# Retention scores from whole float32 q and k, one head in each half of the array's rows

## The chip, the cores and the metric

The kernel runs on one core of one Trainium2 chip. The metric is the device time of one execution in microseconds (us). Before the change it is 1157.19 us, the median of three runs (1155.11 to 1158.36). A single run differs from another by about 0.3%.

## The reference

Three layers follow each other on 4608 tokens (8 sequences of 576) with 512 features (8 heads of 64):

```python
# retention: q, k, v are (8, 8, 576, 64)
scores = scale * np.matmul(q, k.transpose(0, 1, 3, 2))
Dmat = np.where(rel >= 0, gamma[:, None, None] ** rel, 0.0)     # rel = row - column
attn_out = np.matmul(scores * Dmat, v)
# experts: each token goes to the one expert with the largest logit
logits = x @ w_gate                                             # 512 -> 8
out[mask] = gate_w[mask, None] * (np.maximum(x[mask] @ w1[e], 0) @ w2[e])   # 512 -> 1024 -> 512
# SoLU layer
h = x @ w_in; solu = h * softmax(h); ln = layernorm(solu) * g_ln; result = ln @ w_out
```

## The kernel before, in words

The program has three stages: retention with gating and routing (about the first 250 us of the span), the experts, and the SoLU layer. The change touches the first stage only.

**Chunks.** Each sequence is cut into five chunks: four of 128 tokens (c = 0 to 3) and one of 64 (c = 4), so there are 40 chunks, numbered n. Retention runs in its chunked form. Within a chunk, the scores are k times q, multiplied by a table of decays (`dt_t`), and then by v. What came before the chunk enters through a 64x64 state per head, the sum of k times v over the earlier chunks, which is multiplied by a decayed q (`qp`). Heads are handled in four pairs: partitions 0 to 63 hold the features of the first head of a pair, 64 to 127 those of the second.

**load(n)**, L395, brings k and q (features on the partitions: `kc[:, KT]`, `kc[:, Q]`), and k and v (tokens on the partitions: `KR`, `VR`) into one tile `kc` of 1 MB. Five such tiles exist. The loads stand in the one queue of SP, and load(n+5) is asked for at the end of chunk n.

**parts(n)**, L416, makes the scores' operands. ScalarE rounds k to float32r (L427) and q to float32r (L429, two instructions, one for each half of the partitions). GpSimd subtracts k's rounded part from k (L430), VectorE q's from q (L432, two instructions). The parts of q go to `qz`, where the columns of one head hold zeros on the partitions of the other, so that one product over 128 rows gives both heads of a pair side by side. Chunks of 64 tokens have whole float32 q with zeros (`q4z`), and are not split.

**prep(n)**, L435, multiplies `KR` by its decay (L442) and makes `qp` (L449, L453), both on GpSimd.

**scores(n)**, L459: for each pair three products (rounded with rounded, rounded with rest, rest with rounded), L477, into half a bank-sized tile `ps`; after two pairs VectorE multiplies by the decay (L478) into `pp`. There are two `ps` tiles of one bank, so the products of the next half wait until L478 has read the one before the last.

**chunk(n)**, L485: `pp` times v into `po` (L494, one head in each half of the columns), the old state times `qp` added to it (L498, 128x128 with zeros outside each head's block), ScalarE copies `po` to `xts` (L506); then k times v for the pair (L511, the two blocks off the diagonal are not used), and VectorE adds the diagonal blocks to the state in SBUF (L517 for c = 0, L519).

**xtile(t)**, L525: a tile of 128 tokens is transposed and multiplied by the gate in one product per feature block (L536), two halves, each copied by ScalarE (L537). After five tiles **route(g)** is put on a list; **tick** hands out some of its small VectorE and ScalarE steps in each chunk. They pick the expert, count places, and scale the rows, which are then stored to memory.

The order on each engine is the order in which the program issues. The main loop (L699) issues for chunk n: scores(n+1), prep and parts of n+3, chunk(n), xtile, some routing steps, load(n+5); for n = 0 and 1 chunk(n) comes ahead of scores(n+1).

Of the kernel before, what the change touches and what calls it, by code (L numbers as in the profile page):

```python
# [43 lines left out]
def mk_consts():  # L44
# [4 lines left out]
    dtab = dtab.transpose(1, 0, 2)  # L49
# [30 lines left out]
def layouts(q, k, v, moe_w_gate, moe_w1, moe_w2, moe2_w_in, moe2_w_out, moe2_g_ln):  # L80
# [8 lines left out]
    def cut(a):  # L89
# [9 lines left out]
        "kt4": kt[:, :, :, n4:].reshape(B, P, -1),  # L99
        "v4": vr[:, n4:],  # L100
        "q4": qt[:, :, :, n4:].reshape(B, P, -1),
# [20 lines left out]
def kernel(ctx: ExitStack, tc, kvc, kt4, v4, q4, wg, w12, win, wout, gln,  # L122
# [60 lines left out]
    def onehots(pool, ts, ncol=NCOL, pid="pid"):  # L183
        """Per token of the tiles ts: its slot's place in a column, and its column with the token's number."""
# [41 lines left out]
    def sums(pool, a, nm):  # L226
        """Running sums of the experts' numbers in a."""
# [9 lines left out]
    def count(psum):  # L237
        """cnt: tokens per expert."""
# [121 lines left out]
    def gather(e, ts, pool, rows=NT):  # L360
        """The rows of window e's tiles ts."""
# [10 lines left out]
    with ExitStack() as ax:  # L372
        tab = ax.enter_context(tc.tile_pool(name="tab", bufs=1))
        ld = ax.enter_context(tc.tile_pool(name="ld", bufs=5))
        wk = ax.enter_context(tc.tile_pool(name="wk", bufs=2))
        ps_s = ax.enter_context(tc.tile_pool(name="ps_s", bufs=2, space=PSUM))
        ps_o = ax.enter_context(tc.tile_pool(name="ps_o", bufs=2, space=PSUM))
        ps_u = ax.enter_context(tc.tile_pool(name="ps_u", bufs=1, space=PSUM))
        ps_x = ax.enter_context(tc.tile_pool(name="ps_x", bufs=2, space=PSUM))

        NQ = 4
        NN = B * NCH
        dt_t = tab.tile([P, H, P], F32, name="dt_t")
# [3 lines left out]
        qz = [tab.tile([P, 2, NP, 2, P], F32R, name=f"qz{i}") for i in range(NQ)]  # L387
        q4z = [tab.tile([P, NP, 2, S - 4 * P], F32, name=f"q4z{i}") for i in range(2)]
        st = [tab.tile([P, NP, P], F32, name=f"st{i}") for i in range(2)]
# [5 lines left out]
        def load(n):  # L395
# [13 lines left out]
            else:  # L409
                for h2, r in enumerate(HALF):  # L410
                    nc.sync.dma_start(q4z[b % 2][r, :, h2, :], q4[b, r].rearrange("p (r j) -> p r j", r=NP))
                nc.sync.dma_start(kc[:, KT, :NP * cl], kt4[b])
                nc.sync.dma_start(kc[:cl, VR], v4[b])
            chunks[n] = [kc, None, None]

        def parts(n):  # L416
            """k and q of a full chunk in two parts; q with zeros in the place of the pair's other head."""
            if n >= NN:
                return
            b, c = divmod(n, NCH)  # L420
            if c == 4:
                return
            kc = chunks[n][0]
            z = qz[(n - b) % NQ]
            kh = wk.tile([P, 2, DM], F32R, name="kh", bufs=4)
            q = kc[:, Q].rearrange("p (r j) -> p r j", r=NP)
# [4 lines left out]
            for h2, r in enumerate(HALF):  # L431
                V.tensor_tensor(out=z[r, 1, :, h2, :], in0=q[r], in1=z[r, 0, :, h2, :].bitcast(F32), op=ALU.subtract)  # L432
            chunks[n][1] = (kh, z)

        def prep(n):  # L435
# [10 lines left out]
            if c > 0:  # L446
                qp = wk.tile([P, NP, P], F32, name="qp", bufs=4)
                if c < 4:
                    nc.gpsimd.tensor_tensor(out=qp, in0=kc[:, Q].rearrange("p (r j) -> p r j", r=NP),  # L449
                                            in1=qt_t[:, :, o - P:o], op=ALU.mult)  # L450
                else:
                    for h2, r in enumerate(HALF):
                        nc.gpsimd.tensor_tensor(out=qp[r, :, :cl], in0=q4z[b % 2][r, :, h2, :],  # L453
                                                in1=qt_t[r, :, o - P:o - P + cl], op=ALU.mult)
                chunks[n][2] = qp
# [3 lines left out]
        def scores(n):  # L459
# [5 lines left out]
            pp = wk.tile([P, H, P], F32, name="pp")  # L465
            for half in range(2):
                ps = ps_s.tile([P, 4, P], F32, name="ps")
                for i in range(2):
                    pr = 2 * half + i
                    o_ = ps[:cl, 2 * i:2 * i + 2, :cl]  # L470
                    kk = slice(pr * cl, pr * cl + cl)
                    if c == 4:
                        nc.tensor.matmul(o_, kc[:, KT, kk], q4z[b % 2][:, pr], start=True, stop=True)
                    else:
                        kh, z = chunks[n][1]
# [7 lines left out]
        free = []  # L483

        def chunk(n):  # L485
            b, c = divmod(n, NCH)
            o, cl = CHUNKS[c]
            kc, _, qp = chunks.pop(n)
            pp = pt.pop(n)
            po = ps_o.tile([P, NP, P], F32, name="po")  # L490
            for pr in range(NP):
                for h2 in range(2):
                    h = 2 * pr + h2
                    nc.tensor.matmul(po[h2 * D:h2 * D + D, pr, :cl], kc[:cl, VR, h * D:h * D + D], pp[:cl, h, :cl],  # L494
                                     start=(pr == 0), stop=(c == 0 and pr == NP - 1))
# [12 lines left out]
            if c < 4:  # L508
                pu = ps_u.tile([P, NP, P], F32, name="pu")
                for pr in range(NP):  # L510
                    nc.tensor.matmul(pu[:, pr, :], kc[:, KR, pr * P:pr * P + P], kc[:, VR, pr * P:pr * P + P],  # L511
                                     start=True, stop=True)
                old, new = st[(c + 1) % 2], st[c % 2]
                for h2 in range(2):
                    r = slice(h2 * D, h2 * D + D)
                    if c == 0:
                        V.tensor_copy(new[r, :, r], pu[r, :, r])  # L517
                    else:
                        V.tensor_tensor(out=new[r, :, r], in0=pu[r, :, r], in1=old[r, :, r], op=ALU.add)  # L519
# [5 lines left out]
        def xtile(t):  # L525
            g = max(i for i, f in enumerate(gfirst) if f <= t)
            i = t - gfirst[g]
            if i == 0:
                grp[g] = rt.tile([P, GMAX, KD, P + E], F32, name="xr", bufs=2)
            xr = grp[g]  # L530
            x = xts.pop(t)
            for half in range(2):
                px = ps_x.tile([P, 2, P + E], F32, name="px")
                for j in range(2):
                    kb = 2 * half + j
                    nc.tensor.matmul(px[:, j, :], x[:, kb, :], wgi[:, kb, :], start=True, stop=True)  # L536
                nc.scalar.copy(xr[:, i, 2 * half:2 * half + 2, :], px)  # L537
            if i == GROUPS[g] - 1:
# [115 lines left out]
        def tick(budget):  # L654
            """Some of the routing's steps; a step for the tensor engine waits for the next round."""
# [9 lines left out]
        blank = lambda i, h2: qz[i][HALF[1 - h2], :, :, h2, :]  # L665
        G = nc.gpsimd
# [537 lines left out]
```

## Time and profile before

| | |
|---|---|
| median of the runs | 1157.19 us |
| span of the profiled execution, first to last instruction | 1153.2 us |
| TensorE (PE) busy | 1091.0 us, 95% |
| VectorE (DVE) busy | 697.4 us, 60% |
| ScalarE (ACT) busy | 459.8 us, 40% |
| GpSimd (POOL) busy | 271.8 us, 24% |

The page gives no other time of the profiled execution than its span, which is 4.0 us shorter than the median of the runs. In the rows below, "x16" counts the records of a group. A float32 product leaves two records for its one instruction, and so does each loading of weights for it (PEld); a float32r product leaves one. The duration of one record of PE runs from its start to its modelled end and overlaps the next, so the pace of the array is read from one start to the next.

### The profile page before, as it was taken

How to read it: one execution, taken by the hardware profiler on the slowest of the kernel's cores; microseconds unless marked ns; L12 is line 12 of the kernel's file. 1: busy time of each engine (PE TensorE's matmuls, PEld its weight loads, DVE VectorE, ACT ScalarE, POOL GpSimd, SP SyncE). 2: the span in 40 equal slices, each digit the busy share in tenths (PEclk: the TensorE clock that was granted, in tenths of full speed). 3: DMA queues.
4: the chain of work that ended last, by engine and by line, in shares of the span. 5: the costliest groups of instructions: out<-in, count | busy, mean ns of one | idle time of the engine just before them, and what ended most of it. 6: DMA issues, size and time to landing. Idle time of an engine off the chain costs nothing.

```text
span 1153.2 us, 18685 instructions
## 1 busy us (share of the span) xinstructions
PE 1091.0 (95%) x7226; PEld 992.9 (86%) x7226; DVE 697.4 (60%) x1468; ACT 459.8 (40%) x858; POOL 271.8 (24%) x263
## 2 busy tenths in 40 slices
PE   5987989789999999999999999999999999999994
PEld 5877888779999999999999998788888888888873
DVE  8789889876333546555556664655555555555550
ACT  4444645533333333333433442433333343343330
POOL 6555555512771010101010000111111111111111
PEclk9988999999999999999999999999999999999997
DMA  8456666643444343435344332111101111010000
GB/s 292 161 176 200 214 201 211 205 131 112 145 137 148 107 159 130 166 124 176 124 154 145 134 109 78 37 55 47 48 26 55 47 46 55 19 55 28 23 24 29
DMA packets 64509, 130.76 MB, mean 113 GB/s; under 512 B 11904, under 2 KB 40320, under 8 KB 60576
## 3 DMA queue, kind: packets, MB, share of 16 engines
q1 hardware_dynamic: 39792, 101.42, 26.0%
q0 software_dynamic: 7200, 19.46, 5.3%
q10 hardware_dynamic: 17424, 8.65, 2.6%
q8 instruction: 58, 0.95, 0.3%
q14 instruction: 35, 0.29, 0.1%
HBM read 99.82 MB, written 29.68 MB: 112 GB/s over the span
## 4 chain that ended last, share of the span: by engine, by line
PE 72%; DVE 1%; issue 1%; DMA 1%; ACT 1%; POOL 0%; POOLq 0%
PE py L833 19%; PE ph L818 18%; PE phh L990 17%; PE pf L1064 15%; PE ptl L1049 2%; PE px L801 1%; DMA x<-xd,src 0%; DVE ll L1052 0%; DMA out_dram<-o__11605,dst 0%; DMA out_dram<-o__11651,dst 0%; DVE u L1012 0%; DVE nm L1000 0%; ACT lh L1051 0%; DVE u L1035 0%; ACT e__8152 L1015 0%
## 5 line engine op out<-in xcount | busy, mean ns | idle before, releaser
L833 PE MATMUL py<-hh,wh 128*128 128x344 f32 (+7 forms) x512 | 157.7, 308 | 0.0
L833 PE MATMUL py<-hl,wh 128*128 128x344 f32 (+7 forms) x512 | 154.8, 302 | 0.0
L833 PE MATMUL py<-hh,wl 128*128 128x344 f32 (+7 forms) x512 | 154.6, 302 | 0.0
L1052 DVE TENSOR_TENSOR ll<-ptl,lh 128x512 fp32r<-128x512 f32 x72 | 49.5, 688 | 105.1 <-ACT lh L1051 105.1
L990 PE MATMUL phh<-wih,yh 128*128 128x512 f32 x272 | 107.4, 395 | 1.2 <-ACT yh L974 1.2
L367 POOL DMA_INDIRECT x<-xd,src x42 | 42.4, 1008 | 277.5 <-PE px L801 216.4
L990 PE MATMUL phh<-wih,yl 128*128 128x512 f32 x272 | 106.9, 393 | 0.1
L990 PE MATMUL phh<-wil,yh 128*128 128x512 f32 x272 | 105.6, 388 | 0.0
L1029 POOL TENSOR_TENSOR rd<-v,mhalf 128x1 f32<-128x1 f32 x36 | 20.4, 565 | 356.1 <-DVE v L1027 356.1
L820 ACT ACTIVATE hh<-ph 128x344 fp32r<-128x344 f32 (+7 forms) x128 | 54.3, 425 | 121.0 <-PE ph L818 118.6
L833 PEld LDWEIGHTS py<-hh,wh 128*128 128x128 f32 x512 | 96.5, 188 | 0.1
L833 PEld LDWEIGHTS py<-hh,wl 128*128 128x128 f32 x512 | 96.5, 189 | 0.0
L833 PEld LDWEIGHTS py<-hl,wh 128*128 128x128 f32 x512 | 96.2, 188 | 0.0
L818 PE MATMUL ph<-xh,wh 128*128 128x344 f32 (+7 forms) x512 | 93.0, 303 | 1.1 <-ACT xh L804 1.1
L818 PE MATMUL ph<-xl,wh 128*128 128x344 f32 (+7 forms) x512 | 93.0, 304 | 0.0
L818 PE MATMUL ph<-xh,wl 128*128 128x344 f32 (+7 forms) x512 | 92.8, 303 | 0.0
L477 PE MATMUL ps<-qz,kh 128*128 128x256 f32 x384 | 60.7, 311 | 30.7 <-DVE pp L478 19.2
L821 DVE SCALAR_TENSOR_TENSOR hl<-ph,hh 128x344 fp32r<-128x344 f32 (+7 forms) x128 | 60.2, 472 | 48.3 <-ACT hh L820 48.0
L178 DVE TENSOR_TENSOR wl<-raw,wh 128x1024 fp32r<-128x1024 f32 x64 | 78.2, 1221 | 17.7 <-ACT wh L177 17.6
L835 ACT COPY yo<-py 128x344 f32<-128x344 f32 (+7 forms) x64 | 26.5, 413 | 142.3 <-PE py L833 111.9
L477 PEld LDWEIGHTS ps<-qz,kh 128*128 128x128 f32 x384 | 53.7, 211 | 33.3 <-issue 13.0
L1064 PE MATMUL pf<-wol,lh 128*128 128x512 f32 x288 | 81.2, 404 | 0.0
(751 smaller groups left out, 2344.0 us busy)
## 6 DMA issues: line engine op xcount, KB each, us to landing
raw<-in_w_dram SPq DMA_DIRECT2D x64, 512.0 KB, 3.5
kc<-in_kvc_dram SPq DMA_DIRECT2D x30, 1024.0 KB, 5.2
xd<-xr ACTq DMA_DIRECT2D x33, 256.0 KB, 4.6
yg<-yd SPq DMA_DIRECT2D x44, 192.0 KB, 2.9
f<-in_win_dram SPq DMA_DIRECT2D x8, 512.0 KB, 4.5
f<-in_wout_dram SPq DMA_DIRECT2D x8, 512.0 KB, 4.3
kc<-in_kvc_dram SPq DMA_DIRECT2D x4, 512.0 KB, 6.3
yd<-yo SPq DMA_DIRECT2D x4, 344.0 KB, 2.4
```

Of the source, the lines that this page charges most:

```text
L178: V.tensor_tensor(out=wl, in0=raw, in1=wh.bitcast(F32), op=ALU.subtract)
L367: nc.gpsimd.indirect_dma_start(out=x[:w, i, :], out_offset=None, in_=xd[:rows, :], in_offset=bass.IndirectOffsetOnAxis(ap=src[:w, e * CT + ...
L477: nc.tensor.matmul(o_, kh[:, a, kk], z[:, w, pr], start=(m == 0), stop=(m == 2))
L818: nc.tensor.matmul(ph, w[:, w0 + kb * P:w0 + kb * P + P], xx[:, kb, cc], start=(n == 0), stop=(n == 3 * KD - 1))
L820: nc.scalar.activation(out=hh[:, cc], in_=ph, func=AF.Relu)
L821: V.scalar_tensor_tensor(out=hl[:, cc], in0=ph, scalar=0.0, in1=hh[:, cc].bitcast(F32), op0=ALU.max, op1=ALU.subtract)
L833: nc.tensor.matmul(p, w[:, ff], h[:, cc], start=(n == 0), stop=(n == 3 * NFB - 1))
L835: nc.scalar.copy(yo[:, cc], p)
L990: nc.tensor.matmul(p[:, half, :], a[:, kb, :], w[:, kb, half * DM:half * DM + DM], start=(kb == 0 and n == 0), stop=(kb == KD - 1 and n == 2))
L1049: nc.tensor.transpose(p[:, kb, :], u[:, f * P:f * P + P], ident)
L1052: V.tensor_tensor(out=ll[:, fs, :], in0=p, in1=lh[:, fs, :].bitcast(F32), op=ALU.subtract)
L1064: nc.tensor.matmul(pfs[t], a[:, f, :], w[:, f, :], start=(n == 0), stop=(n == m - 1))
```

## The change

The scores are computed from k and q as they are loaded, in float32. For each pair two products take the place of three: the first head on rows 0 to 63 of the array, the second on rows 64 to 127 (`r` below), with no zeros anywhere. The two heads' scores of a chunk of 128 go to two banks (`ps[:, h2]`), and one VectorE instruction multiplies the whole chunk. With that parts, its ten kinds of tiles with zeros, and the clearing of them go. In the chunk of 64 the heads also lie one in each half of the partitions.

The state is summed over the chunks in PSUM (`pu` is kept over a sequence, 64 columns for a head) and copied out by one VectorE instruction; its product with `qp` is 64 by 64 for a head. `po` and the gate's `px` have one buffer each instead of two, `ps` has two buffers of two banks. Seven `kc` tiles instead of five are there, and load(n+7) is issued at the end of chunk n. The two halves of xtile are issued apart, one before chunk(n) and one behind it, and k times v comes ahead of the state's product.

```diff
-        ld = ax.enter_context(tc.tile_pool(name="ld", bufs=5))
+        ld = ax.enter_context(tc.tile_pool(name="ld", bufs=7))
-        ps_o = ax.enter_context(tc.tile_pool(name="ps_o", bufs=2, space=PSUM))
+        ps_o = ax.enter_context(tc.tile_pool(name="ps_o", bufs=1, space=PSUM))
-        ps_x = ax.enter_context(tc.tile_pool(name="ps_x", bufs=2, space=PSUM))
+        ps_x = ax.enter_context(tc.tile_pool(name="ps_x", bufs=1, space=PSUM))
...
-                nc.sync.dma_start(kc[:, KT, :NP * cl], kt4[b])
-                nc.sync.dma_start(kc[:cl, VR], v4[b])
+                nc.sync.dma_start(kc[:, :2, :NP * cl], kq4[b].rearrange("p (a f) -> p a f", a=2))
+                nc.sync.dma_start(kc[:, VR, :NP * D], v4[b])
...
-            nc.scalar.copy(kh[:, 0], kc[:, KT])
-            for h2, r in enumerate(HALF):
-                (V.tensor_copy if n == 0 else nc.scalar.copy)(z[r, 0, :, h2, :], q[r])
-            (V if n in (2, 3) else nc.gpsimd).tensor_tensor(out=kh[:, 1], in0=kc[:, KT], in1=kh[:, 0].bitcast(F32), op=ALU.subtract)
-            for h2, r in enumerate(HALF):
-                V.tensor_tensor(out=z[r, 1, :, h2, :], in0=q[r], in1=z[r, 0, :, h2, :].bitcast(F32), op=ALU.subtract)
...
-                        for m, (a, w) in enumerate(((0, 0), (0, 1), (1, 0))):
-                            nc.tensor.matmul(o_, kh[:, a, kk], z[:, w, pr], start=(m == 0), stop=(m == 2))
-                V.tensor_tensor(out=pp[:cl, 4 * half:4 * half + 4, :cl], in0=ps[:cl, :, :cl],
-                                in1=dt_t[:cl, 4 * half:4 * half + 4, :cl], op=ALU.mult)
+            ps = ps_s.tile([P, 2, NP, P], F32, name="ps")
+            for pr in range(NP):
+                kk = slice(pr * cl, pr * cl + cl)
+                for h2, r in enumerate(HALF):
+                    o_ = ps[:, h2, pr, :] if c < 4 else ps[r, 0, pr, :cl]
+                    nc.tensor.matmul(o_, kc[r, KT, kk], kc[r, Q, kk], start=True, stop=True)
+            if c < 4:
+                V.tensor_tensor(out=pp, in0=ps, in1=dtc, op=ALU.mult)
+            else:
+                V.tensor_tensor(out=pp[:, 0, :, :cl], in0=ps[:, 0, :, :cl], in1=dt4, op=ALU.mult)
...
+            if c < 4:
+                if c == 0:
+                    sums_[0] = ps_u.tile([P, NP, D], F32, name="pu")
+                pu = sums_[0]
+                for pr in range(NP):
+                    for h2, r in enumerate(HALF):
+                        h = 2 * pr + h2
+                        nc.tensor.matmul(pu[r, pr, :], kc[:, KR, h * D:h * D + D], kc[:, VR, h * D:h * D + D],
+                                         start=(c == 0 and pr == 0), stop=(pr == NP - 1), skip_group_check=True)
+                V.tensor_copy(new, pu)
             if c > 0:
                 for pr in range(NP):
-                    nc.tensor.matmul(po[:, pr, :cl], st[(c + 1) % 2][:, pr, :], qp[:, pr, :cl], start=False, stop=(pr == NP - 1))
+                    for r in HALF:
+                        nc.tensor.matmul(po[r, pr, :cl], old[r, pr, :], qp[r, pr, :cl], start=False, stop=(pr == NP - 1))
...
-                    if c == 0:
-                        V.tensor_copy(new[r, :, r], pu[r, :, r])
-                    else:
-                        V.tensor_tensor(out=new[r, :, r], in0=pu[r, :, r], in1=old[r, :, r], op=ALU.add)
...
+            scores(n + 1)
+            prep(n + 2)
+            ready = (nx + 1) * P <= b * S + CHUNKS[c][0]
+            if ready:
+                xtile(nx, 0)
             chunk(n)
...
+            if ready:
+                xtile(nx, 1)
                 nx += 1
...
-            load(n + 5)
+            load(n + 7)
```

The table of decays grows from 512 KB to 640 KB, since the chunk of 64 has its own copy; the bytes of a chunk of 64 stay 384 KB, in two transfers instead of four.

On TensorE, this stands before in a row for the third and fourth chunk of the second sequence (`ps` scores, `po` output, `pu` k times v, `px` gate):

```order
L477 MATMUL ps<-qz_129,kh 128x256 x12
L494 MATMUL po<-pp,kc 64x128 x8
L498 MATMUL po<-qp,st_133 128x128 x4
L511 MATMUL pu<-kc 128x128 x4
L536 MATMUL px<-wgi,xts 128x136 x4
L473 MATMUL ps<-q4z_131,kc 64x2x64 x4
```

At the same place after the change there stands this:

```order
L445 MATMUL ps<-kc 128x128 x8
L507 MATMUL px<-wgi,xts 128x136 x2
L467 MATMUL po<-pp,kc 64x128 x8
L475 MATMUL pu<-kc 64x64 x8
L481 MATMUL po<-qp,st_127 64x128 x8
L507 MATMUL px<-wgi,xts 128x136 x2
L445 MATMUL ps<-kc 64x64 x8
```

Twelve score products of 256 columns became eight of 128, k times v and the state went from four products to eight narrower ones in the other order, and the gate's products stand in two places.

On VectorE, this stands before in a row for the last chunks of the first sequence:

```order
L478 TENSOR_TENSOR pp<-ps,dt_t 128x512 x2
L432 TENSOR_TENSOR qz_126<-kc,qz_126 64x4x128 x2
L519 TENSOR_TENSOR st_132<-pu,st_133 64x4x64 x2
L478 TENSOR_TENSOR pp<-ps,dt_t 64x4x64 x2
L432 TENSOR_TENSOR qz_127<-kc,qz_127 64x4x128 x2
L519 TENSOR_TENSOR st_133<-pu,st_132 64x4x64 x2
```

After the change the same chunks have this:

```order
L447 TENSOR_TENSOR pp<-ps,dt_t 128x1024
L477 COPY st_127<-pu 128x256
L447 TENSOR_TENSOR pp<-ps,dt_t 128x1024
L477 COPY st_126<-pu 128x256
L449 TENSOR_TENSOR pp<-ps,dt_t 128x4x64
L477 COPY st_127<-pu 128x256
```

Six instructions for a chunk became two, and nothing stands between a chunk's `pp` and its state any more.

## Rows read from the trace of the kernel before

**Rows 1.** Busy time by stretch: time, each engine, clock, DMA share, GB/s

```profile
0.00:240.00 240.00, 202.15 (x1899) 185.85 (x1900) 207.49 (x383) 116.92 (x242) 131.63 (x113) 0.95 0.63 205
265.00:1153.00 888.00, 867.33 (x5172) 786.78 (x5170) 472.31 (x1013) 331.32 (x591) 134.35 (x144) 0.99 0.26 88
```

**Rows 2.** Waits of PE in 0 to 250: total, times, longest

```profile
PE ps L477 <- DVE pp L478: 19.2, 9, 6.3
PE ps L477 <- DVE qz L432: 4.9, 3, 2.9
PE po L498 <- DVE st L517: 3.1, 4, 1.2
PE po L498 <- DVE st L519: 1.8, 1, 1.8
```

**Rows 3.** Groups of instructions by line and shape, 0 to 265

```profile
L432 DVE TENSOR_TENSOR qz<-kc,qz 64x512 fp32r<-64x512 f32 x64 | 72.6, 1134 | 5.2 <-ACT qz L429 3.7
L478 DVE TENSOR_TENSOR pp<-ps,dt_t 128x512 f32<-128x512 f32 x64 | 41.6, 685 | 5.4 <-PE ps L477 4.9
L430 POOL TENSOR_TENSOR kh<-kc,kh 128x512 fp32r<-128x512 f32 x30 | 41.2, 1374 | 55.0 <-ACT kh L427 52.3 <-DMA kc<-in_kvc_dram 2.7
L429 ACT CAST qz<-kc 64x512 fp32r<-64x512 f32 x62 | 38.2, 616 | 0.8
L519 DVE TENSOR_TENSOR st<-pu,st 64x256 f32<-64x256 f32 x48 | 20.2, 420 | 11.7 <-PE pu L511 8.2 <-PE pcnt L240 2.7
L427 ACT CAST kh<-kc 128x512 fp32r<-128x512 f32 x32 | 19.8, 617 | 13.3 <-DMA kc<-in_kvc_dram 13.0
L517 DVE COPY st<-pu 64x256 f32<-64x256 f32 x16 | 6.7, 422 | 0.4
L478 DVE TENSOR_TENSOR pp<-ps,dt_t 64x256 f32<-64x256 f32 x16 | 6.2, 412 | 1.1 <-PE ps L473 0.9
```

**Rows 4.** PE in order of time, 231 to 244: start, duration, group

```profile
231.31 1.70 PE L477 MATMUL ps<-qz,kh 128*128 128x256 f32 x12 [2.18 <-DVE pp L478]
232.94 1.09 PE L494 MATMUL po<-pp,kc 128*64 128x128 f32 x16
233.96 1.16 PE L498 MATMUL po<-qp,st 128*128 128x128 f32 x8
234.96 1.06 PE L511 MATMUL pu<-kc 128*128 128x128 f32 x8
235.85 1.09 PE L536 MATMUL px<-wgi,xts 128*128 128x136 f32 x8
236.78 0.38 PE L202 MATMUL pm<-m,m 128*128 128x96 bf16 x5
237.08 0.98 PE L473 MATMUL ps<-q4z,kc 128*64 128x128 f32 x7
...
237.96 1.09 PE L494 MATMUL po<-pp,kc 128*64 128x128 f32 x15
...
241.99 0.68 PE L494 MATMUL po<-pp,kc 64*64 64x64 f32 x16
242.61 1.10 PE L498 MATMUL po<-qp,st 128*128 128x64 f32 x8
```

**Rows 5.** The first stretch: PE and ACT about 20 us, in order of time

```profile
20.03 0.62 ACT L427 CAST kh<-kc 128x512 fp32r<-128x512 f32 x1 [0.50 <-DMA kc<-in_kvc_dram]
23.19 0.36 PE L477 MATMUL ps<-qz,kh 128*128 128x256 f32 x1 [0.54 <-ACT xr L537]
```

**Rows 6.** DMA queues in 0 to 250: packets, MB, share of 16 engines

```profile
q1 hardware_dynamic: 14448, 41.05, 49.2%
q10 hardware_dynamic: 16368, 8.13, 11.4%
```

**Rows 7.** One stretch of the start, columns as in rows 1

```profile
10.00:20.00 10.00, 9.69 (x75) 8.24 (x74) 9.18 (x12) 4.68 (x8) 7.15 (x5) 1.00 1.08 361
```

More of the change, by code (lines that the diff above doesn't have):

```diff
@@ L121, with kernel @@
 @with_exitstack
-def kernel(ctx: ExitStack, tc, kvc, kt4, v4, q4, wg, w12, win, wout, gln,
+def kernel(ctx: ExitStack, tc, kvc, kq4, v4, wg, w12, win, wout, gln,
                                    dtab, qtab, ktab, cst, out, dbg=None):
@@ L386 @@
         wgi = tab.tile([P, KD, P + E], F32, name="wgi")
-        qz = [tab.tile([P, 2, NP, 2, P], F32R, name=f"qz{i}") for i in range(NQ)]
-        q4z = [tab.tile([P, NP, 2, S - 4 * P], F32, name=f"q4z{i}") for i in range(2)]
-        st = [tab.tile([P, NP, P], F32, name=f"st{i}") for i in range(2)]
+        st = [tab.tile([P, NP, D], F32, name=f"st{i}") for i in range(2)]
         KT, Q, KR, VR = range(4)
@@ L409, in load @@
             else:
[L410 to L433 removed]
+                nc.sync.dma_start(kc[:, :2, :NP * cl], kq4[b].rearrange("p (a f) -> p a f", a=2))
+                nc.sync.dma_start(kc[:, VR, :NP * D], v4[b])
+            chunks[n] = [kc, None]
         def prep(n):
@@ L447, in prep @@
                 qp = wk.tile([P, NP, P], F32, name="qp", bufs=4)
-                if c < 4:
-                    nc.gpsimd.tensor_tensor(out=qp, in0=kc[:, Q].rearrange("p (r j) -> p r j", r=NP),
-                                            in1=qt_t[:, :, o - P:o], op=ALU.mult)
-                else:
[L452 to L455, printed above, removed]
+                nc.gpsimd.tensor_tensor(out=qp[:, :, :cl], in0=kc[:, Q, :NP * cl].rearrange("p (r j) -> p r j", r=NP),
+                                        in1=qt_t[:, :, o - P:o - P + cl], op=ALU.mult)
+                chunks[n][1] = qp
         pt = {}
@@ L464, in scores @@
             kc = chunks[n][0]
[L465 to L475, printed above, removed]
-                        for m, (a, w) in enumerate(((0, 0), (0, 1), (1, 0))):
-                            nc.tensor.matmul(o_, kh[:, a, kk], z[:, w, pr], start=(m == 0), stop=(m == 2))
-                V.tensor_tensor(out=pp[:cl, 4 * half:4 * half + 4, :cl], in0=ps[:cl, :, :cl],
-                                in1=dt_t[:cl, 4 * half:4 * half + 4, :cl], op=ALU.mult)
+            pp = wk.tile([P, 2, NP, P], F32, name="pp")
+            ps = ps_s.tile([P, 2, NP, P], F32, name="ps")
[8 more added lines that the diff above has]
+                V.tensor_tensor(out=pp[:, 0, :, :cl], in0=ps[:, 0, :, :cl], in1=dt4, op=ALU.mult)
             pt[n] = pp
         xts = {}
-        free = []
+        sums_ = [None]
         def chunk(n):
@@ L507, in chunk @@
                 a += w
[L508 to L515, printed above, removed]
-                    if c == 0:
-                        V.tensor_copy(new[r, :, r], pu[r, :, r])
-                    else:
-                        V.tensor_tensor(out=new[r, :, r], in0=pu[r, :, r], in1=old[r, :, r], op=ALU.add)
             tick(1.0)
@@ L523, with xtile @@
         grp = {}
-        def xtile(t):
+        def xtile(t, half):
             g = max(i for i, f in enumerate(gfirst) if f <= t)
             i = t - gfirst[g]
-            if i == 0:
+            if i == 0 and half == 0:
                 grp[g] = rt.tile([P, GMAX, KD, P + E], F32, name="xr", bufs=2)
             xr = grp[g]
[L531 to L538, printed above, removed]
+            x = xts[t] if half == 0 else xts.pop(t)
+            px = ps_x.tile([P, 2, P + E], F32, name="px")
+            for j in range(2):
+                kb = 2 * half + j
+                nc.tensor.matmul(px[:, j, :], x[:, kb, :], wgi[:, kb, :], start=True, stop=True)
+            nc.scalar.copy(xr[:, i, 2 * half:2 * half + 2, :], px)
+            if half == 1 and i == GROUPS[g] - 1:
                 todo.append(route(g))
@@ L689 @@
         load(4)
-        parts(0)
-        V.memset(st[0], 0.0)
-        V.memset(st[1], 0.0)
+        load(5)
+        load(6)
         prep(0)
         scores(0)
-        parts(1)
         prep(1)
@@ L701 @@
             held[0] = False
-            if n > 1:
-                scores(n + 1)
-                for i in ((4, 5) if n == 2 else (n + 3,)):
-                    prep(i)
-                    parts(i)
-            done = b * S + CHUNKS[c][0]
+            scores(n + 1)
[3 more added lines that the diff above has]
+                xtile(nx, 0)
             chunk(n)
-            if n < 2:
-                scores(n + 1)
-                prep(n + 2)
-                parts(n + 2)
             if n == 0:
@@ L715 @@
                 V.tensor_copy(tri, C("tri"))
-            if (nx + 1) * P <= done:
-                xtile(nx)
+            if ready:
+                xtile(nx, 1)
                 nx += 1
@@ L729 @@
         while nx < NTT:
-            xtile(nx)
+            xtile(nx, 0)
+            xtile(nx, 1)
             nx += 1
```

39 lines of the change are left out of this document (15 added, 24 removed).

## Prediction

> **What bounds the kernel now.** I read the busy time by stretch first, since the change touches only the first 250 us. From 265 us on PE is busy for 867 of 888 us [rows 1]: that part is the array's, and no edit reaches it. In the first 240 us PE is busy for 202 and VectorE for 207, 86% of the time, so two engines share the bound there. The waits of PE come next: 19.2 us in which the scores' products wait until VectorE has emptied a `ps` tile (longest 6.3 us), 4.9 us for its splitting of q, 4.9 us for the state in SBUF [rows 2]. The groups by line say what VectorE does meanwhile: 72.6 of its 207 us are the subtractions of L432 [rows 3]. PE in order of time, in a stretch with hardly a wait, gives the price of each step, from one start to the next [rows 4]. The granted clock of 0.95 in the first 240 us [rows 1], with full and half speed as its two levels (2.4 and 1.2 GHz), means some 24 us at half, 12 us of work lost.
>
> So the reader is to see a stage in which PE has less work than time. One full chunk costs PE [rows 4]: scores 1.63 us (231.31 to 232.94), output 1.02, state 1.00, k times v 0.89, gate 0.93 (235.85 to 236.78), together 5.47. The first chunk of a sequence has no state product: 4.47. The chunk of 64: scores 0.88 (237.08 to 237.96), output 0.62, state 0.94 (its 1.10 less the 0.16 by which the 1.16 above stands over its pace of 1.00), gate 0.93: 3.37. A sequence: 3 x 5.47 + 4.47 + 3.37 - 0.47 (4.5 gate tiles for five chunks) = 23.8, eight of them 190. Until the scores of the fourth chunk start at 23.19 [rows 5], 10.6 are done (three scores, two outputs, two k times v, a state, a gate tile); behind the last chunk's state product, which ends at 242.61 + 1.10 = 243.7, 1.9 are left (two gate tiles). So 177.5 us of work take 220.5, and 43 us go to waits and to the low clock.
>
> **The change part by part.** *VectorE.* L432 (72.6), both forms of L478 (41.6 and 6.2), L519 (20.2) and L517 (6.7) go, 147 us. There come 32 products of 1024 columns: 128x512 takes 0.685 and 64x256 0.412, so 0.273 for each 256 columns more, 1.23 us each, 39 us; eight of 256 columns, 3.3 us; 32 copies of 256 columns at 0.42, 13.4 us [rows 3]. Of 207 us about 116 stay.
>
> *ScalarE and GpSimd.* L429 and L427 go, 58 of 117 us; L430 goes, 41 of 132 us [rows 1, 3]. Neither is late for PE today, so by itself this is worth nothing; it keeps both below the shorter stage. The clearing of the tiles with zeros lies beside the first load: nothing.
>
> *PE.* Nothing in this trace puts two products into the two halves of the array's rows. The nearest row is L494, which puts two heads into the two halves of the columns: 16 records of 128 columns, 1.02 us. L473 has 8 records of the same shape, all in one half, and takes 0.88 [rows 4]. So column halves run beside each other. If row halves do too, eight score products (16 records) take 1.02 like L494; if not, 16 records at 0.11 (L511, eight in 0.89) take 1.78 and a change of shape. I take the overlap, since shape and count are L494's turned by a quarter, and keep the other end for the range.
>
> A change of the operands' shape costs about 0.12: the same eight records take 1.00 behind L494 and 0.89 without a change [rows 4]. The old order has two changes in a full chunk, the new one five, all counted in the terms that follow: scores 1.02; first gate half 0.93 / 2 + 0.12 = 0.59; output 1.02; k times v, 16 records of 64x64, which the chunk of 64 does in 0.62 with a change, 0.50 without; state 1.02 (two heads on the diagonal); second gate half 0.59. Together 4.74, without state 3.72. The chunk of 64: 0.62 + 0.59 + 0.62 + 0.50 + 0.59 = 2.92. A sequence: 3 x 4.74 + 3.72 + 2.92 - 0.59 = 20.3, eight 162. Less 8.3 done at the fourth chunk's scores and 1.8 behind the end: 152.
>
> *The start.* The fourth chunk's k lands at 20.03 [rows 5]; the transfers are the bound until then (361 GB/s [rows 7]). The larger decay table, 128 KB ahead of them, adds 0.4 us at that rate. Its scores no longer wait for splitting, so they start at 20.4, not 23.2.
>
> *Waits.* The new order gives `pp` of the next chunk the whole of chunk(n), some 3.7 us, to be made in 1.23; L477's copy has as long. What is late next is ScalarE: `px` has one buffer, and the copy of its second half stands behind `xts` and, once per group of tiles, behind scalings that wait for VectorE. PE waits then, with all that is queued behind the gate's product. I take a third of the 43 us as staying, 14, since VectorE goes from 86% to about 116 of 170 us, 68%. Bounds: none stay, or all 43. The last gate tile pays 0.7 us for the single buffer.
>
> *Loads.* Seven tiles instead of five let loads run two chunks further ahead; they hang on `kc` being free, not on PE's waits. They cost nothing while the engines have room (a rival below). The routing's steps keep their places per chunk.
>
> The sum: 20.4 + 152 + 14 = 186.5 for the end of the last state product, against 243.7: 57.2 less, with the 0.7 at the tail 56.5. The profiled span goes from 1153.2 to 1096.7. The median of the runs stands 4.0 above the span, so **1100**. With no waits 1086, with all 43 it is 1129.
>
> **The rivals.** *Row halves do not overlap, at the scores or at the state.* The scores then cost 16 x 0.11 + 0.12 = 1.9 instead of 1.02, 0.9 x 32 = 29 us more: 1129. Where both halves write one bank at once, as the state's product (`po`) and the three products of the chunk of 64 do, a bar to the overlap costs 0.89 x 24 + 3 x 0.44 x 8 = 32: 1132. For overlap: L494's column halves write one bank, each on its partitions, at full pace. Against: no row has two row halves. One of the two 0.14; both 0.06, 1161, the gain is gone.
>
> On this the Trainium skill speaks against the change: TensorEngine Tiling (Array Packing), section "Gotcha 1: PSUM Pressure", has it that "different row tiles cannot access same PSUM bank simultaneously" and leaves the order to the program; by it the 32 us just worked out would be paid. The same skill, TensorE: Matmul & The Clock Gate, section "Part 3: Packing small matmuls — row/col tiling", says that products on separate row groups run at once; by it the forecast stands. No row here shows either.
>
> *Each change of row half is a change of shape (slower).* Heads alternate in the new loops, so if the array empties at each change of half as it does at a change of shape, 16 records at 0.11 gain seven times 0.12, at scores and state alike: (0.9 + 0.84) x 56 sets and half of it at 24 small ones, 118 us more: 1218. It decides from about 0.1 us per record of the new products: 57 us over 1280 records (32 and 24 sets of 16, 24 small ones) is 45 ns over the forecast's 55. Against it stands the same alternation of column halves in L494, which costs nothing. Chance 0.05.
>
> *The transfers become the bound.* The two queues take 60.6% of the 16 engines in 250 us, 151 us of full use [rows 6]; in 186 us that is 81%, where the stage has 0.63 now [rows 1] and 1.08 while they are pressed [rows 7]. If no more than 0.70 comes out, with stores in bursts beside the loads, the stage ends at 216: 1130. For it: 0.63 is what waiting queues use. Against: the start. Chance 0.08.
>
> *All waits stay*, since routing and not the splits holds VectorE up: 1129, chance 0.05. 19.2 + 4.9 + 4.9 of the waits name VectorE's split, `pp` and state [rows 2], all of which shrink.
>
> **How the numbers follow.** Forecast 0.62, one overlap missing 0.14, transfers 0.08, all waits 0.05, no overlap 0.06, emptying 0.05. The likeliest gives 1100, by itself 1086 to 1115. The range takes in the cases at 1129 to 1132 and a little below the case without waits: 1082 to 1134. A measurement of this kernel tells 0.3%, 3.5 us, from no change. Faster by more: 0.62 + 0.14 + 0.08 + 0.05 = 0.89. The case without any overlap lies at the edge: 0.04 same, the rest slower, 0.07 with the emptying.
>
> **What would show it.** Right: L445 in starts two at a time, its 16 records in about 1.0 us; the last L481 ending at 180 to 195; VectorE near 120 us in the stage; no PE wait for `pp`; a granted clock near 1.00 from 20 us on; PE's time from there to the end as before. Wrong: records of L445 or L481 0.11 apart (no overlap); PE waiting for `kc` or GpSimd with the DMA share flat at 0.7 to 0.8 (transfers); ScalarE's copies of `px` as PE's main releaser beyond 15 us (waits).

## The result: 1125.68 us, a gain of 32 us where 57 were forecast

| | before | after | forecast |
|---|---|---|---|
| median of four runs of each, us | 1157.78 | 1125.68 | 1100 |
| ratio, with its 95% interval | | 0.9724 (0.9708 to 0.9739) | 0.951 |
| span of the profiled execution, us | 1153.2 | 1124.6 | 1096.7 |
| fourth chunk's scores start, us | 23.19 | 21.56 | 20.4 |
| last state product ends, us | 243.70 | 213.34 | 186.5 |

The time is faster and inside the range, but above the likeliest case's own range (1086 to 1115). The last two rows place the miss: the start is 1.2 us late, and the stage behind it takes 191.8 us instead of 166.1. The busy time by stretch, in the columns of [rows 1], answers to [rows 1, 7] (line numbers below are those of the changed kernel, where nothing else is said):

```profile
10.00:20.00 10.00, 8.20 (x102) 7.50 (x104) 4.15 (x5) 0.97 (x2) 5.22 (x5) 1.00 1.07 371
0.00:210.00 210.00, 176.38 (x2603) 154.73 (x2605) 108.40 (x240) 62.78 (x147) 71.73 (x68) 0.96 0.70 235
265.00:1124.00 859.00, 840.92 (x5005) 761.09 (x5003) 453.40 (x959) 320.68 (x572) 126.14 (x136) 0.99 0.26 87
21.56:213.34 191.78, 167.41 (x2514) 146.48 (x2514) 104.67 (x246) 61.51 (x149) 65.87 (x59) 0.96 0.66 222
```

The second row shows VectorE at 108 us (forecast 116) and ScalarE and GpSimd at about half of what they were; behind 265 us PE is busy for 98% of the time, as before. The last row is the stage from the fourth chunk's scores to the last state product. PE idles for 191.8 less 167.4, 24.4 us, and a clock of 0.96 means some 15 us at half speed, at most 7.7 us of work lost (at most, since some of it falls on idle time). The same row of the kernel before:

```profile
23.19:243.70 220.51, 191.56 (x1839) 176.82 (x1840) 190.63 (x368) 107.14 (x229) 115.82 (x94) 0.95 0.59 192
```

There 29.0 us are idle and at most 11.0 lost to the clock. So waits and clock went from 40 only to 32 us, while the work went from 180.5 to 159.7 (busy time less what the clock lost). That the waits are not the old ones is seen in the waits of PE after, 0 to 235 us, in the columns of [rows 2]:

```profile
PE px L507 <- ACT xr L508: 24.8, 12, 7.3
PE ps L445 <- DMA kc<-in_kvc_dram: 9.7, 3, 4.8
PE px L507 <- ACT xts L489: 2.0, 1, 2.0
```

The waits for `pp`, for the split of q and for the state are gone (19.2, 4.9 and 4.9 us in [rows 2]). In their place PE waits 24.8 us for ScalarE's copy of the gate's `px`. The wait for `kc` lies in the start, ahead of the fourth chunk.

The groups of instructions by line and shape, after, answer to [rows 3]: what came for L432, L478, L519 and L517, and the new products.

```profile
L447 DVE TENSOR_TENSOR pp<-ps,dt_t 128x1024 f32<-128x1024 f32 x32 | 39.0, 1220 | 29.3 <-PE ps L445 21.1 <-DMA dt_t<-in_dtab_dram 8.1
L445 PE MATMUL ps<-kc 64*128 64x128 f32 x512 | 39.0, 294 | 9.7 <-DMA kc<-in_kvc_dram 9.7
L481 PE MATMUL po<-qp,st 64*64 64x128 f32 x384 | 28.2, 289 | 0.0
L477 DVE COPY st<-pu 128x256 f32<-128x256 f32 x32 | 13.5, 422 | 44.8 <-PE pu L475 44.8
```

VectorE now waits for PE (21.1 and 44.8 us), no longer the other way round. PE in order of time, after, in a stretch without a wait, columns as in [rows 4]:

```profile
21.56 1.16 PE L445 MATMUL ps<-kc 64*128 64x128 f32 x16
22.65 0.73 PE L507 MATMUL px<-wgi,xts 128*128 128x136 f32 x4
23.31 1.09 PE L467 MATMUL po<-pp,kc 128*64 128x128 f32 x16
24.24 0.63 PE L475 MATMUL pu<-kc 128*64 128x64 f32 x16
24.80 1.09 PE L481 MATMUL po<-qp,st 64*64 64x128 f32 x16
25.82 0.73 PE L507 MATMUL px<-wgi,xts 128*128 128x136 f32 x4
26.48 0.68 PE L445 MATMUL ps<-kc 64*64 64x64 f32 x16
27.09 0.73 PE L507 MATMUL px<-wgi,xts 128*128 128x136 f32 x4
...
32.68 0.68 PE L467 MATMUL po<-pp,kc 64*64 64x64 f32 x16
33.19 0.63 PE L481 MATMUL po<-qp,st 64*64 64x64 f32 x16
33.76 0.73 PE L507 MATMUL px<-wgi,xts 128*128 128x136 f32 x4
```

From start to start a full chunk takes 4.92 us (21.56 to 26.48; forecast 4.74): scores 1.09, gate half 0.66, output 0.93, k times v 0.56, state 1.02, gate half 0.66. Of the chunk of 64, scores take 0.61, output 0.51 and state 0.57. Sixteen records in 1.09 or 1.02 us are the pace of overlapping row halves.

Here is the longest stop, PE and ScalarE in order of time after the change; ACTq rows are DMAs that ScalarE's queue issues, and brackets give an engine's idle time just before and what ended it:

```profile
166.76 0.73 PE L507 MATMUL px<-wgi,xts 128*128 128x136 f32 x4
...
167.04 0.52 ACTq L559 DMA_DIRECT2D xd<-xr  x1
167.41 0.72 ACT L551 ACTIVATE xr<-xr,gt 128x512 f32<-128x512 f32 x1
...
167.42 1.16 PE L445 MATMUL ps<-kc 64*128 64x128 f32 x16
...
167.65 7.76 ACTq L559 DMA_DIRECT2D xd<-xr  x4
...
175.46 0.39 ACT L508 COPY xr<-px 128x272 f32<-128x272 f32 x1 [7.32 <-DMA xd<-xr]
...
175.89 1.27 PE L507 MATMUL px<-wgi,xts 128*128 128x136 f32 x4 [7.32 <-ACT xr L508]
```

The second half of one gate tile is done by 167.5 (the next chunk's scores follow it). Its copy (L508) stands in ScalarE's queue behind five stores of the scaled rows (L559), and to issue the last four takes 7.76 us. `px` has one buffer, so the next tile's first gate product waits until 175.89, and everything of PE's that is queued behind it. The clock falls too, late in the stop; the stretches of the stop and behind it (columns as in [rows 1]):

```profile
168.00:176.00 8.00, 0.69 (x13) 0.49 (x9) 3.58 (x4) 0.52 (x2) 1.98 (x2) 0.86 0.94 305
176.00:180.00 4.00, 4.00 (x38) 3.63 (x40) 0.03 (x1) 0.39 (x1) 0.00 (x0) 0.50 0.28 83
```

PE is fully busy from 176 to 180, at 0.50. In the stop PE is busy for 0.69 of 8 us, ScalarE for 0.52, GpSimd for 1.98 and VectorE for 3.58, while the DMA engines are 94% busy.

### The profile page after: what moved, and what is told of

Same layout as the page of the kernel before. It is cut to its first block, busy times and chain, and to the rows that moved or that the text cites. A ratio compares the mean times of both kernels' runs of the same rounds, so it can differ in the third digit from the quotient of the medians.

```text
span 1124.6 us, 19711 instructions
## 1 busy us (share of the span) xinstructions
PE 1065.6 (95%) x7930; PEld 961.8 (86%) x7930; DVE 596.9 (53%) x1323; ACT 405.3 (36%) x762; POOL 213.1 (19%) x218
## 4 chain that ended last, share of the span: by engine, by line
PE 74%; DVE 1%; issue 1%; DMA 1%; ACT 1%; POOL 0%; POOLq 0%
PE py L785 19%; PE ph L770 18%; PE phh L942 17%; PE pf L1016 16%; PE ptl L1001 3%; PE px L753 1%; DMA x<-xd,src 1%; DVE ll L1004 0%; DMA out_dram<-o__11361,dst 0%; DMA out_dram<-o__11407,dst 0%; DVE u L964 0%; DVE nm L952 0%; ACT lh L1003 0%; DVE u L987 0%; POOL rd L981 0%
## 5 line engine op out<-in xcount | busy, mean ns | idle before, releaser
L981 POOL TENSOR_TENSOR rd<-v,mhalf 128x1 f32<-128x1 f32 x36 | 20.4, 566 | 356.1 <-DVE v L979 356.1
L770 PEld LDWEIGHTS ph<-xh,wh 128*128 128x128 f32 x512 | 78.4, 189 | 1.2 <-ACT xh L756 1.2
L507 PE MATMUL px<-wgi,xts 128*128 128x136 f32 x288 | 53.6, 310 | 26.9 <-ACT xr L508 24.8
L770 PEld LDWEIGHTS ph<-xl,wh 128*128 128x128 f32 x512 | 78.6, 189 | 0.1
```

The source lines that it names most:

```text
L770: nc.tensor.matmul(ph, w[:, w0 + kb * P:w0 + kb * P + P], xx[:, kb, cc], start=(n == 0), stop=(n == 3 * KD - 1))
L981: nc.gpsimd.tensor_tensor(out=rd, in0=v, in1=mhalf, op=ALU.pow)
```

## Experiments

My theory was that ScalarE's stores hold the one `px` buffer. The rivals: the single buffer alone, the number of loads in flight, VectorE's load, and the summing in PSUM as a gain of its own; the question of the row halves was still to be tested by itself. The runs came in three sets, each on a chip of its own (e1 to e4, e5 to e8, e9 to e12), and every kernel is longer there than in the result: the kernel before takes 1199.80, 1198.97 and 1201.54 us. Early in the experts stage PE also waits there for "issue", that is for nothing that the profile shows: 29.7 us from 225 to 345 us in e5, none in the result's trace. So ratios to the kernel before on the same chip are compared, and in the traces the stage: from the fourth chunk's scores to the end of the last state product. The stage differs less from chip to chip: 191.8 us in the result and 196.1 in e5 for the changed kernel, 220.5 and 222.8 (e10) for the old one. The table is read from one row of busy time for each kernel, like the two above; idle is the length less PE's busy time.

| run | edit to the changed kernel | ratio (95%) | start, us | stage, us | PE busy | idle | clock |
|---|---|---|---|---|---|---|---|
| e1 | stores in SP's queue | 0.9568 (0.9521 to 0.9615) | 21.16 | 165.3 | 160.5 | 4.7 | 1.00 |
| e2 | two `px`, one `ps` | 0.9598 (0.9546 to 0.9649) | 22.79 | 176.0 | 164.7 | 11.3 | 0.97 |
| e3 | row halves apart | 0.9890 (0.9841 to 0.9938) | 22.46 | 203.6 | 187.0 | 16.6 | 0.95 |
| e4 | five `kc` tiles | 0.9734 (0.9686 to 0.9781) | 21.78 | 188.7 | 168.8 | 19.9 | 0.95 |
| e5 | none | 0.9816 (0.9783 to 0.9849) | 22.79 | 196.1 | 169.5 | 26.6 | 0.94 |
| e6 | e1 and e2 | 0.9544 (0.9518 to 0.9570) | 22.38 | 168.1 | 161.7 | 6.5 | 0.99 |
| e7 | 64 subtractions added to VectorE | 0.9878 (0.9853 to 0.9904) | 27.08 | 196.5 | 170.8 | 25.7 | 0.95 |
| e8 | state summed in SBUF | 0.9818 (0.9788 to 0.9848) | 22.77 | 194.0 | 168.8 | 25.3 | 0.95 |
| e9 | e1 again | 0.9571 (0.9530 to 0.9612) | 22.06 | 166.3 | 160.4 | 5.9 | 1.00 |
| e11 | e1 and e7 | 0.9715 (0.9674 to 0.9756) | 27.80 | 177.6 | 163.5 | 14.1 | 0.99 |
| e12 | e1 and e4 | 0.9576 (0.9533 to 0.9619) | 21.70 | 167.3 | 160.5 | 6.8 | 1.00 |

**e1, the stores in SP's queue.**

```diff
-                        nc.scalar.dma_start(xd[(f + i) * P:(f + i + 1) * P, :].rearrange("p (k d) -> p k d", k=KD), xr[:, i, :, :P])
+                        nc.sync.dma_start(xd[(f + i) * P:(f + i + 1) * P, :].rearrange("p (k d) -> p k d", k=KD), xr[:, i, :, :P])
```

> The changed kernel (1125.7 us) with the stores of the scaled rows to memory (L559) issued from SP's queue instead of ScalarE's. Theory S (stores): five stores in a row hold ScalarE for 3.6 to 7.8 us, the copy of the gate's second half stands behind them, and the array waits because px has one buffer. Then the five long waits (4.6, 2.1, 2.6, 7.5 and 3.1 us) go, and some of the low clock behind them: 1100 to 1108 us, PE's wait for L508 falls from 25 us to under 10. Rival R (routing): the copy stands behind scalings that wait for VectorE; the stores are beside the point: 1123 to 1127. Rival D (transfers): the engines are full, and the wait turns up at kc: 1123 to 1128.

1147.65 us, 0.9568, which is 1108 us where the kernel before takes 1157.78: the upper end of theory S. The waits of PE for L508 in the stage of the changed kernel, 21 to 214 us, nearly all of its 24.4 us of idle time:

```profile
PE px L507 <- ACT xr L508: 21.9, 10, 7.3
```

The waits of PE in e1, 21 to 187 us:

```profile
PE px L507 <- ACT xr L508: 4.3, 7, 0.9
PE po L467 <- DVE tm L534: 0.4, 1, 0.4
```

And the same place of a group of tiles, in order of time (SPq: issued by SP's queue):

```profile
52.75 3.69 SPq L559 DMA_DIRECT2D xd<-xr  x5
52.89 0.72 ACT L551 ACTIVATE xr<-xr,gt 128x512 f32<-128x512 f32 x1
53.05 0.73 PE L507 MATMUL px<-wgi,xts 128*128 128x136 f32 x4 [0.88 <-ACT xr L508]
53.81 0.39 ACT L508 COPY xr<-px 128x272 f32<-128x272 f32 x1 [0.20 <-PE px L507]
```

The five issues still take 3.69 us, but ScalarE copies `px` beside them, and no wait is longer than 0.9 us. Idle time and low clock are nearly gone, as the rows of the stage show, e1 first and the changed kernel (e5) second:

```profile
21.16:186.41 165.25, 160.52 (x2515) 140.51 (x2515) 103.93 (x246) 61.01 (x149) 66.64 (x60) 1.00 0.75 259
22.79:218.90 196.11, 169.53 (x2514) 148.56 (x2514) 104.73 (x246) 61.17 (x149) 64.05 (x58) 0.94 0.63 214
```

One line of the program holds back some 30 us of the stage: 196.1 to 165.3 between these two, which ran on two chips, and 196.1 to 168.1 on one chip (e5 and e6, which has e2's edit too).

**e2, two buffers of `px`** (paid for with one of `ps`).

```diff
-        ps_s = ax.enter_context(tc.tile_pool(name="ps_s", bufs=2, space=PSUM))
+        ps_s = ax.enter_context(tc.tile_pool(name="ps_s", bufs=1, space=PSUM))
...
-        ps_x = ax.enter_context(tc.tile_pool(name="ps_x", bufs=1, space=PSUM))
+        ps_x = ax.enter_context(tc.tile_pool(name="ps_x", bufs=2, space=PSUM))
```

> The changed kernel with two px buffers, and one ps buffer of two banks to make room. S and R alike: with a second buffer the array meets ScalarE's lateness only when it is over some 4 us (most of a chunk), so nearly all the waits for L508 go: 1098 to 1106 us; the longest stop of ScalarE (7.8 us) still shows under S. With one ps buffer the scores wait for pp only if VectorE is more than about 2 us late. D: no gain, PE waits for kc instead: 1123 to 1128.

1153.61 us, 0.9598; on the scale of the result's chip 1111 us, more than the 1098 to 1106 expected. A second buffer bridges most stops of ScalarE but not the longest; two waits on it remain (5.1 us), and 5.9 us come for the single `ps`. So it takes both, the stores ahead of the copy and the single buffer, to stop PE. **e6** joins it with e1:

> The changed kernel with both: stores from SP's queue, two px buffers and one ps buffer. Theory S, that both act on one cause (ScalarE late with the copy of px): little beyond the better of the two, since with the stores gone the waits left for L508 are 9 us, of which a second buffer takes most: 0.950 to 0.956 of before. If they acted on two causes, their gains would add: about 0.944.

1144.99 us, 0.9544, not told apart from e1 and e9. The two edits remove the same waits: with the stores gone, what the second `px` still saves (e9 waits 5.2 us for it) comes back as waits for the single `ps` (6.4 us).

**e3, the row halves apart.** The loop over halves goes outside that over pairs.

```diff
-            for pr in range(NP):
-                kk = slice(pr * cl, pr * cl + cl)
-                for h2, r in enumerate(HALF):
+            for h2, r in enumerate(HALF):
+                for pr in range(NP):
+                    kk = slice(pr * cl, pr * cl + cl)
```

> The changed kernel with the score products of the four first heads issued ahead of those of the four second heads, so that neighbours in the queue use the same half of the rows. If the gain at the scores is the overlap of the two halves of the rows, the 16 records take 0.11 us each instead of 0.055: L445's group of 16 goes from 1.16 to about 2.0 us, 0.85 us in 32 chunks and 0.44 in 8, 31 us, of which the present waits for ScalarE hide up to 10: 1143 to 1157. If the overlap does not hang on the order, or the scores are not on the path: 1124 to 1128.

1187.19 us, 0.989. The group of the scores in e3, by line and shape:

```profile
L445 PE MATMUL ps<-kc 64*128 64x128 f32 x512 | 57.8, 295 | 8.3 <-DMA kc<-in_kvc_dram 8.3
```

The fourth chunk's scores in e3, in order of time:

```profile
22.46 1.71 PE L445 MATMUL ps<-kc 64*128 64x128 f32 x16
24.10 0.73 PE L507 MATMUL px<-wgi,xts 128*128 128x136 f32 x4
```

From the first start to the second, 1.64 us. The same 512 records take 57.8 us instead of 39.0, a chunk's 1.64 instead of 1.09 us. So the pace of the alternating order is the overlap of the halves. Beside e5 (on another chip) the busy time grows by 17.5 us but the stage by only 7.5, since idle time shrinks by 10: part of the longer work falls into what was waiting for ScalarE. Against e5's ratio the loss is some 9 us, less than the 17 to 31 expected: a chunk's scores grew by 0.55 us, not by 0.85.

**e4, five `kc` tiles.**

```diff
-        ld = ax.enter_context(tc.tile_pool(name="ld", bufs=7))
+        ld = ax.enter_context(tc.tile_pool(name="ld", bufs=5))
...
-        load(5)
-        load(6)
...
-            load(n + 7)
+            load(n + 5)
```

> The changed kernel with five kc tiles and loads five chunks ahead, as before. If the depth itself pays (loads late without it), PE waits for kc by 5 to 15 us more: 1131 to 1141. If five are enough at 5 us a chunk: 1124 to 1127. If the deep loads are what presses the stores (S with contention), their issue gets shorter with fewer loads in flight, and the time falls to 1115 to 1122.

1168.69 us, 0.9734: beside e5, on another chip, faster by 0.8% of the time before, with intervals that only just do not meet; the result's ratio, 0.9724, is no worse. The traces show shorter stops: 19.9 us idle (26.6 in e5, 24.4 in the result), and the last four issues of the longest row take 5.92 us in e4 and 7.96 in e5. The first row of stores, e4 and then e5:

```profile
56.67 3.50 ACTq L559 DMA_DIRECT2D xd<-xr  x4
57.27 5.01 ACTq L559 DMA_DIRECT2D xd<-xr  x4
```

That fewer loads in flight leave the stores more room is the likely reading. **e12** has both edits, e1 and this one:

> The stores from SP with five kc tiles. In e4 five tiles were 10 us better than seven beside stores from ScalarE, by shorter stops of ScalarE. If that was all, the depth is worth nothing here: within 3 us of e9. If SP, now with the stores in its queue ahead of the loads, is late with them, seven tiles pay: e12 5 to 12 us slower than e9.

1148.72 us, 0.9576, beside e9's 0.9571. Without stores in ScalarE's queue the number of tiles is worth nothing, so whatever e4 gained came through the shorter stops.

**e5, the changed kernel again**, as a yardstick for these chips.

> The changed kernel itself, as the yardstick for the other kernels of this set, since chips differ by some per cent: 0.972 to 0.975 of the kernel before.

1178.88 us, 0.9816, outside the 0.972 to 0.975 expected: here the change gains 20 us, not 32. In its stage idle time and clock lose 6 us more than in the result's trace; 1 more is the later start, and where the other 5 go stays open.

**e7, work back on VectorE.** Two subtractions of 64x512 for each full chunk, whose results nothing reads.

```diff
+                scr = wk.tile([P, DM], F32, name="scr")
+                for r in HALF:
+                    V.tensor_tensor(out=scr[r], in0=kc[r, Q], in1=kc[r, KT], op=ALU.subtract)
```

> The changed kernel with the load of the old splitting put back on VectorE alone: two subtractions of 64x512 per chunk of 128, in the place where q was split, into a tile that nothing reads; some 70 us in all. Theory V (VectorE's load was what held the array before): the waits for VectorE come back, 15 to 30 us of the 32 gained are lost, ratio 0.984 to 0.998. Rival P (the gain is the array's own shorter work and the loads that come earlier): within 4 us of the changed kernel, ratio 0.971 to 0.977.

1184.77 us, 0.9878, 6 us behind e5 on the same chip, between the two theories. The subtractions put back less than the 70 us expected, by the group of them from 0 to 225 us:

```profile
L423 DVE TENSOR_TENSOR scr<-kc 64x512 f32<-64x512 f32 x64 | 53.4, 834 | 9.4 <-DMA kc<-in_kvc_dram 9.0
```

The stage's length is that of e5 (196.5 and 196.1); the loss is the later start, 27.08 against 22.79, since these subtractions make VectorE wait for a load there, with `pp` behind them. **e11** puts the same work beside e1's stores:

> The stores from SP, and 70 us of subtractions put back on VectorE. In e7 they cost 6 us, but there ScalarE's stops were in the way and could hide VectorE's lateness. Theory V: with the stops gone VectorE's load is felt, the stage ends 10 to 25 us later than in e9. Rival P: the chunk-long lead of pp hides it, as in e7: 0 to 6 us later, and the new order of the work, not the lighter VectorE, took the old waits away.

1165.76 us, 0.9715, 17 us behind e9. Of these 5.7 lie in the start and 11.3 in the stage. The waits of PE in e11, 22 to 205 us (its lines stand three further on):

```profile
PE px L510 <- ACT xr L511: 9.4, 7, 3.0
PE pu L478 <- DVE st L480: 2.8, 4, 0.9
PE po L470 <- DVE pp L450: 0.9, 2, 0.5
```

VectorE's load counts here, in part through ScalarE, whose scalings wait for it (14.0 us for `gt`, 7.7 in e9). In the changed kernel its effect on the stage is hidden behind the stops of ScalarE. Taking the splitting off VectorE is therefore worth something to the stage, but only once the stores have moved. The stage's row in e11:

```profile
27.80:205.40 177.60, 163.54 (x2514) 141.96 (x2514) 151.16 (x302) 60.70 (x148) 65.07 (x56) 0.99 0.65 225
```

VectorE is busy for 85% of it, as much as in the old kernel (190.6 of 220.5 us, 86%). Yet PE waits for VectorE only 3.7 us (2.8 and 0.9), where the old kernel's waits for it were 29 [rows 2]. So the old waits stay away in the new kernel even with VectorE busy for the old share of the time. The new order, with `pp` a chunk ahead, or the fewer steps on VectorE between a chunk's scores and its state can be what keeps them away; no run tells these two apart.

**e8, the state summed in SBUF** as before, with the new products.

```diff
-                if c == 0:
-                    sums_[0] = ps_u.tile([P, NP, D], F32, name="pu")
-                pu = sums_[0]
+                pu = ps_u.tile([P, NP, D], F32, name="pu")
...
-                                         start=(c == 0 and pr == 0), stop=(pr == NP - 1), skip_group_check=True)
-                V.tensor_copy(new, pu)
+                                         start=(pr == 0), stop=(pr == NP - 1))
+                if c == 0:
+                    V.tensor_copy(new, pu)
+                else:
+                    V.tensor_tensor(out=new, in0=pu, in1=old, op=ALU.add)
```

> The changed kernel with the state summed in SBUF again: the sum in PSUM starts anew in each chunk, and VectorE adds it to the old state (one instruction of 128x256, as long as the copy that it replaces). If summing in PSUM is worth nothing by itself: ratio as the changed kernel, within 2 us. If the longer chain over VectorE is felt: 3 to 8 us slower.

1178.01 us, 0.9818, as e5. The addition takes VectorE 423 ns, the copy 422, and VectorE waits for PE ahead of either. Beside the stops of ScalarE, then, summing in PSUM is worth nothing by itself; with the stores moved it was not tried.

**e9, e1 again**, on the chip of e10 to e12.

> The changed kernel with the stores from SP's queue once more (as e1), as the yardstick of this set: 0.953 to 0.960 of the kernel before, the last state product of the stage at about 186 us.

1148.88 us, 0.9571. e1 repeats.

**e10, the kernel before with its stores in SP's queue** (its L588, the edit of e1).

> The kernel before with its stores (L588) issued from SP's queue. If the stores held the array there too, it gains 5 us or more, and part of e1's gain is not the change's. Theory S says no: ScalarE is held 3 to 5 us per five stores there as well, but the gate's px has two buffers and q and k are rounded three chunks ahead, and PE waits for L537 only 1.0 us: within 3 us of the kernel before, ratio 0.997 to 1.003.

1203.80 us, 1.0025 (1.0004 to 1.0046): nothing gained. The waits of PE in it, 22 to 246 us:

```profile
PE ps L477 <- DVE pp L478: 19.8, 9, 6.2
PE po L498 <- DVE st L517: 4.6, 4, 2.1
PE ps L477 <- DVE qz L432: 3.9, 1, 3.9
```

They are those of [rows 2]. The old kernel had the same stores in the same queue and did not wait for them; the change made them count. They also took less time to issue there: at the median 0.62 us for one, at most 1.61, against 0.76 and 2.43 in the changed kernel.

## Why the forecast missed by 26 us

The direction was right and the time lies inside the range, but only because the range was drawn wide enough for rivals at 1129 to 1132. Their causes did not come, so that it fell inside is luck. By spans the miss is 27.9 us: 26.8 at the last state product, and 1.1 behind it, where 911.3 us are left after and 909.5 before, with 0.7 allowed for. In the medians it is 26, because span and median lie 1.1 us apart after the change and not 4.0.

**The start** came at 21.56 instead of 20.4. Small, and not tested.

**The array's work.** By the same measure it was 180.5 us and is 159.7, so 20.8 less; the working had 177.5 and 152, 25.5 less. The scores, output, k times v and state together take 3.60 a chunk against 3.56 in the working. In e1 and e9, where the clock is full, PE is busy for 160.5 and 160.4, which bears the 159.7 out. What was short is the gate: 0.66 each half instead of 0.59, 72 times, 5 us. The change of shape around it costs nearer 0.2 than 0.12 there (0.66 less 0.47).

**The overlap of the row halves**, the term on which most chance outside the forecast lay, was right: 1.09 and 1.02 us for the sixteen records of scores and state, 0.61, 0.51 and 0.57 in the short chunk (0.62, 0.62 and 0.50 in the working), and e3 shows what it is worth: 0.55 us a chunk, less than the 0.9 at which the rival was priced. The state's product and the short chunk's put both halves into one bank and run at the same pace. The sentence of the Trainium skill, TensorEngine Tiling (Array Packing), "Gotcha 1: PSUM Pressure", that stood against the change cost nothing here: its 32 us did not come, with the halves on partitions of their own.

**The waits: the step that failed.** It read "I take a third of the 43 us as staying, 14, since VectorE goes from 86% to about 116 of 170 us". VectorE did go to 105 of 192, and the waits for it did go, though e11 shows them gone at 85% as well, so VectorE's share was no measure for them. But idle time and low clock make 32 us, not 14. The working had named the place ("What is late next is ScalarE: `px` has one buffer"), and put it behind `xts` and the scalings only; it gave no price to the five stores that ScalarE issues in the same place, and scaled the old waits by VectorE's load, which has no part in the new one. The sign that the prediction gave for this error is the one that came: `px` copies as PE's main releaser beyond 15 us (24.8). The size of the rival "all waits stay" (1129) came near, but not its cause: routing holds ScalarE, not VectorE. Two of the prediction's signs of being right failed with it: the last L481 ends at 213, not at 180 to 195, and the clock in the stage is 0.96, not near 1.00. With the stores moved (e1) the stage ends at 186.4, by accident the forecast's 186.5: waits of 5 instead of 14, work of 160 instead of 152.

**The transfers.** The two queues in 0 to 215 us after, columns as in [rows 6]:

```profile
q1 hardware_dynamic: 11632, 41.18, 55.0%
q10 hardware_dynamic: 15840, 7.87, 12.4%
```

Together they use 67% of a shorter stretch, 145 us of full use, about what they did. They were not the bound: without the stops the stage runs at a DMA share of 0.75 (e1's row, 259 GB/s), above the 0.70 of that rival. They matter only through the time that a store takes to issue.

So of 27 us that the stage ends late, 1 is the start, 8 are work (5 of them the gate; the other 3 are in the old kernel's row as well, 180.5 against the 177.5 added up), and 18 waits and clock. The last are the stores in ScalarE's queue: e1 and e9 leave 4.7 and 5.9 us idle at a full clock, and e10 shows that they cost nothing while VectorE held the array.

The best version run is the changed kernel with its stores in SP's queue: 0.957 of the kernel before (0.954 with e2's edit as well, not told apart), where the changed kernel has 0.982 in e5.

## What to carry to other kernels

When a bound engine is freed, price the next one by what stands in its queue in order, DMA issues included, ahead of the instruction that is waited for; don't scale the old waits. An engine that frees a single-buffered PSUM tile is a poor place to issue stores from while loads press the DMA engines. And an edit that is worth nothing while another wait covers it (VectorE's load, e7 and e11) has to be tried again when that wait is gone.

## What was not expected of the hardware

Issuing a 256 KB store held ScalarE's queue for about 0.5 us in the best case (0.52) and 1.9 us on average in the longest row (7.76 for four), while the sixteen DMA engines were 94% busy. The Trainium skill, DMA: Bandwidth & Descriptors, "Issuing engines are not separate DMA queues", says that issuing from several engines saves only the sequencer's time, usually small beside the transfer. For a single store this case agrees (0.76 us at the median beside 6.5 us from its issue to landing); but four issues in the longest row took longer than one store takes to land, and taking them off ScalarE was worth some 30 us of the stage.

Beyond that, a wait of 7.3 us was followed by half the clock on a fully busy PE (0.50 from 176 to 180 us), so that this stop cost more than its length.
